# Linear attention beside a GEGLU block: heads packed in chunks of 120 columns against chunks of 128, with the first steps of two engines in program order

## The chip, the cores and the metric

The kernel runs on one core of a Trainium2 chip. The time is device time in microseconds (us) of whole executions; the profile shows one execution, and its span is about 1.8 us shorter than the time. Five engines matter. TensorE multiplies matrices (PE in the profile, its weight loads are PEld), VectorE (DVE) and ScalarE (ACT) do elementwise work, the Pool engine (POOL) helps, and SyncE (SP) starts the DMAs. All runs told of here are in the fast state. Ratios are the mean time of one kernel's fast runs over that of the other's of the same rounds, so they are not quite the ratio of the medians quoted beside them.

## The reference

```python
x  = A_x                                  # 1 x 2048 x 640, bf16
xn = layernorm(x)
# A: linear attention, 32 heads of 20
q, k, v = split(xn @ wqkv)                # 640 -> 3 * 640
pq, pk  = phi(q), phi(k)                  # phi(t) = where(t > 0, t + 1, exp(t)) + 1e-6
kv = sum over tokens of pk^T v            # per head, 20 x 20
z  = sum over tokens of pk                # per head, 20
o  = (pq @ kv) / (pq @ z + 1e-6)
A  = o @ wo
# B: GEGLU
B  = (gelu(xn @ w_gate) * (xn @ w_up)) @ w_down   # 640 -> 1728 -> 640
out = x + A + B
```

## The kernel before

The kernel has two stages. The k/v stage goes through 16 tiles of 128 tokens: statistics and normalization, five transposes, k and v by matmuls, phi(k), and the sum of pk^T v in an accumulator. Then come four blocks of 512 tokens: q and phi(q), 13 gate/up chunks and one tail chunk, with the attention of the block (nd, its division, transposes) put between the first chunks, then the last projection.

Heads of 20 columns don't fill 128 evenly. So the kernel before takes six heads at a time, 120 columns, and the last 40 columns of the 640 as a sixth chunk:

```python
HPC = P // Dh            # 6 heads
CW = HPC * Dh            # 120 columns
HC = -(-D // CW)         # 6 chunks
NW = CW + HPC            # 126
...                      # HCH: (lo, m, voff, vw) of each chunk; the last one is widened to 128 columns

def kv_accumulate(t, pk, v_ext):
    for j, (lo, m, voff, vw) in enumerate(HCH):
        col = (j % GPB) * P
        nc.tensor.matmul(
            kv_acc[0:m, j // GPB, col:col + 1 + vw],
            lhsT=pk[:, lo:lo + m], rhs=v_ext[:, j, 0:1 + vw], ...)
...
for i in range(NT + 2):                  # the k/v stage, pipelined over tiles
    if i < NT:
        ensure_stats(i)                  # bn_stats on VectorE, log and exp on ScalarE, in batches:
        normalize_transpose(i)           #   tile 0, tile 1, tiles 2-3, tiles 4-5, ...
    if 0 <= i - 1 < NT:
        pk = k_tile(i - 1); v_ext = v_tile(i - 1); ...
    if 0 <= i - 2 < NT:
        kv_accumulate(i - 2, ...)
...
def nd_tile(b, tt, pqT):                 # numerators and denominators of one token tile
    nd = ps_nd.tile([P, HC, P], FP32, tag="nd")          # ps_nd has one buffer
    for j, (lo, m, voff, vw) in enumerate(HCH):
        nc.tensor.matmul(nd[:, j, 0:NW], lhsT=pqT[0:m, j, tsl], rhs=kvz[0:m, j, :], ...)
    # VectorE: rden = nd[.., CW:] + eps; rden = 1 / rden; o = nd * rden   (720 columns)
...
    for j, (lo, m, voff, vw) in enumerate(HCH):          # q of a block: 6 chunks
        for c in range(DC):
            nc.tensor.matmul(q_ps[0:m, :], lhsT=wqkv_sb[:, c, lo:lo + m], rhs=xnT[:, c, bsl], ...)
        phi(pqT[0:m, j, :], q_ps[0:m, :], m, TB, "eq")
```

The order of instructions on each engine is not that of the text: a scheduler orders them, from its own estimate of when each is ready.

Of the kernel before, what the change touches and what calls it, by code (L numbers as in the profile page):

```python
# [8 lines left out]
ALU = mybir.AluOpType  # L9
FP32 = mybir.dt.float32  # L10
BF16 = mybir.dt.bfloat16
PSUM = bass.MemoryType.PSUM
# [4 lines left out]
DEN_EPS = 1e-6  # L17
# [6 lines left out]
def kernel(  # L24
# [11 lines left out]
    nc = tc.nc  # L36
    P = nc.NUM_PARTITIONS

    Bsz, S, D = A_x.shape
    F = B_w_gate.shape[1]  # L40
    H = N_HEADS
    Dh = D // H
    assert Bsz == 1 and D % P == 0 and D == H * Dh
    TB = 512
    assert S % TB == 0
    DC = D // P
    NT = S // P
    NB = S // TB
    TPB = TB // P
    HPC = P // Dh  # L50
    CW = HPC * Dh
    HC = -(-D // CW)
    NW = CW + HPC

    HCH = []
    for j in range(HC):
        lo = j * CW
        vw = min(CW, D - lo)
        if vw <= 64 and D >= P:
            HCH.append((D - P, P, P - vw, vw))  # L60
        else:
            HCH.append((lo, vw, 0, vw))

    n_plain = F // P
    f_tail = F - n_plain * P
# [7 lines left out]
    SG = D // NS  # L73

    KA = D // 2
    nA = max(1, (HC + 1) // 2)
    VA = nA * CW
    assert KA <= 512 and D - KA <= 512 and VA <= 512 and 0 < D - VA <= 512
    nfullB = (D - VA) // CW
    tailB = D - VA - nfullB * CW  # L80
    GPB = 3
    assert HC <= 2 * GPB and NW <= P and (CW + 1) <= P

    x_flat = A_x.rearrange("b s d -> (b s) d")
    out_flat = out.rearrange("b s d -> (b s) d")
# [3 lines left out]
    consts = ctx.enter_context(tc.tile_pool(name="consts", bufs=1))  # L89
    wpool = ctx.enter_context(tc.tile_pool(name="wpool", bufs=1))  # L90
    big = ctx.enter_context(tc.tile_pool(name="big", bufs=1))
    blk = ctx.enter_context(tc.tile_pool(name="blk", bufs=1))
# [60 lines left out]
    )  # L153
    eps_ln = consts.tile([P, 1], FP32, name="eps_ln")
    nc.vector.memset(eps_ln[:], LN_EPS)
    masks = {}
    for (lo, m, voff, vw) in HCH:
        if voff in masks:
            continue
        mk = consts.tile([P, HPC, Dh], FP32, name=f"mask{voff}")  # L160
        nc.gpsimd.memset(mk[:], 1.0)
        nc.gpsimd.affine_select(
            out=mk[:], in_=mk[:], compare_op=ALU.is_ge, fill=0.0,
            base=-voff, pattern=[[-Dh, HPC], [0, Dh]], channel_multiplier=1,
        )
        nc.gpsimd.affine_select(
            out=mk[:], in_=mk[:], compare_op=ALU.is_ge, fill=0.0,
            base=voff + Dh - 1, pattern=[[Dh, HPC], [0, Dh]], channel_multiplier=-1,
        )
        masks[voff] = mk  # L170
    kvz = big.tile([P, HC, NW], BF16, name="kvz")
    nc.gpsimd.memset(kvz[:], 0.0)

    xnT = big.tile([P, DC, S], BF16, name="xnT")
# [2 lines left out]
    rstd_all = big.tile([P, NT], FP32, name="rstd_all")  # L177
    nmr_all = big.tile([P, NT], FP32, name="nmr_all")

    kv_acc = ps_nd.tile([P, 2, 512], FP32, tag="nd")  # L180
    nc.vector.memset(kv_acc[:], 0.0)

    def phi(dst, src_ps, rows, cols, tag):
        e = work.tile([P, cols], FP32, tag=tag)
        nc.scalar.activation(out=e[0:rows], in_=src_ps, func=ACT.Exp)  # L185
        nc.vector.tensor_scalar(  # L186
            out=e[0:rows], in0=e[0:rows], scalar1=1.0, scalar2=PHI_EPS,
            op0=ALU.min, op1=ALU.add,
        )
        nc.vector.scalar_tensor_tensor(  # L190
            out=dst, in0=src_ps, scalar=0.0, in1=e[0:rows], op0=ALU.max, op1=ALU.add
        )
# [53 lines left out]
    def v_tile(t):  # L246
        tsl = slice(t * P, (t + 1) * P)
        vA = ps_oa.tile([P, VA], FP32, tag="oa")
        vB = ps_ob.tile([P, D - VA], FP32, tag="ob")
        for (ps, lo, hi) in ((vA, 0, VA), (vB, VA, D)):  # L250
            for c in range(DC):
                nc.tensor.matmul(  # L252
                    ps[:], lhsT=xnT[:, c, tsl], rhs=wqkv_sb[:, c, 2 * D + lo:2 * D + hi],
                    start=(c == 0), stop=(c == DC - 1),
                )
        v_ext = work.tile([P, HC, CW + 1], BF16, tag="vext")
        nc.gpsimd.memset(v_ext[:, :, 0:1], 1.0)
        nc.scalar.copy(
            out=v_ext[:, 0:nA, 1:1 + CW], in_=vA[:].rearrange("p (j c) -> p j c", c=CW)
        )  # L260
        if nfullB:
            nc.scalar.copy(
                out=v_ext[:, nA:nA + nfullB, 1:1 + CW],
                in_=vB[:, 0:nfullB * CW].rearrange("p (j c) -> p j c", c=CW),
            )
        if tailB:
            nc.scalar.copy(out=v_ext[:, HC - 1, 1:1 + tailB], in_=vB[:, nfullB * CW:])
        return v_ext

    def kv_accumulate(t, pk, v_ext):  # L270
        for j, (lo, m, voff, vw) in enumerate(HCH):
            col = (j % GPB) * P
            nc.tensor.matmul(  # L273
                kv_acc[0:m, j // GPB, col:col + 1 + vw],
                lhsT=pk[:, lo:lo + m], rhs=v_ext[:, j, 0:1 + vw],
                start=False, stop=(t == NT - 1), skip_group_check=True,
            )

# [16 lines left out]
        stats_done.add(bi)  # L295

    pend_kv = {}
    for i in range(NT + 2):
        if i < NT:
            ensure_stats(i)  # L300
            normalize_transpose(i)
        if 0 <= i - 1 < NT:
            t = i - 1
            pk = k_tile(t)
            v_ext = v_tile(t)
            pend_kv[t] = (pk, v_ext)
        if 0 <= i - 2 < NT:
            t = i - 2
            kv_accumulate(t, *pend_kv.pop(t))

    for j, (lo, m, voff, vw) in enumerate(HCH):
        g_, col = j // GPB, (j % GPB) * P
        mk = masks[voff]
        mk2d = mk[:].rearrange("p h d -> p (h d)")
        nc.vector.tensor_tensor(
            out=kvz[0:m, j, 0:vw], in0=kv_acc[0:m, g_, col + 1:col + 1 + vw],
            in1=mk2d[0:m, 0:vw], op=ALU.mult,
        )
        nc.vector.tensor_scalar(
            out=kvz[0:m, j, CW:CW + HPC], in0=mk[0:m, :, 0],  # L320
            scalar1=kv_acc[0:m, g_, col:col + 1], scalar2=None, op0=ALU.mult,
        )

    def nd_tile(b, tt, pqT):
        tsl = slice(tt * P, (tt + 1) * P)
        nd = ps_nd.tile([P, HC, P], FP32, tag="nd")
        for j, (lo, m, voff, vw) in enumerate(HCH):
            nc.tensor.matmul(  # L328
                nd[:, j, 0:NW], lhsT=pqT[0:m, j, tsl], rhs=kvz[0:m, j, :],
                start=True, stop=True,  # L330
            )
        rden = small.tile([P, HC, HPC], FP32, tag="rden")
        nc.vector.tensor_scalar(
            out=rden[:], in0=nd[:, :, CW:CW + HPC], scalar1=DEN_EPS, scalar2=None, op0=ALU.add
        )
        nc.vector.reciprocal(out=rden[:], in_=rden[:])
        o = work.tile([P, HC, HPC, Dh], BF16, tag="o")
        nc.vector.tensor_tensor(  # L338
            out=o[:],
            in0=nd[:, :, 0:CW].rearrange("p j (h d) -> p j h d", d=Dh),  # L340
            in1=rden[:].unsqueeze(3).to_broadcast([P, HC, HPC, Dh]),
            op=ALU.mult,
        )
        return o

    def tr_tile(b, tt, o, oT):
        tsl = slice(tt * P, (tt + 1) * P)
        o_flat = o[:].rearrange("p j h d -> p (j h d)")
        oT_ps = ps_tp.tile([P, DC, P], BF16, tag="tp")
        for c in range(DC):  # L350
            nc.tensor.transpose(oT_ps[:, c, :], o_flat[:, c * P:(c + 1) * P], ident[:])  # L351
        nc.scalar.copy(out=oT[:, :, tsl], in_=oT_ps[:])  # L352
# [63 lines left out]
    TR_AT = 3  # L416
    for b in range(NB):
        bsl = slice(b * TB, (b + 1) * TB)
        pqT = blk.tile([P, HC, TB], BF16, tag="pqT")
        for j, (lo, m, voff, vw) in enumerate(HCH):  # L420
            q_ps = ps_mm.tile([P, TB], FP32, tag="mm")
            for c in range(DC):
                nc.tensor.matmul(  # L423
                    q_ps[0:m, :], lhsT=wqkv_sb[:, c, lo:lo + m], rhs=xnT[:, c, bsl],
                    start=(c == 0), stop=(c == DC - 1),
                )
            phi(pqT[0:m, j, :], q_ps[0:m, :], m, TB, "eq")
        oT = blk.tile([P, DC, TB], BF16, tag="oT")
        hT = blk.tile([P, FC, TB], BF16, tag="hT")
        o_tiles = {}  # L430
        for fc in range(FC):
            ffn_chunk(b, fc, hT)
            last = (fc == FC - 1)
            for tt in range(TPB):
                if fc == ND_AT + tt or (last and tt not in o_tiles and fc < ND_AT + tt):
                    o_tiles[tt] = nd_tile(b, tt, pqT)
            for tt in range(TPB):
                if tt in o_tiles and o_tiles[tt] is not None and (fc == TR_AT + tt or last):
                    tr_tile(b, tt, o_tiles[tt], oT)
                    o_tiles[tt] = None  # L440
        for tt in range(TPB):
            final_tile(b, tt, hT, oT)
# [30 lines left out]
```

## Time and profile before

| | before |
|---|---|
| time | 306.18 us median (305.46 to 307.96, 16 runs) |
| TensorE busy | 294.4 of 304.7 us (97%) |
| k/v stage ends, first q matmul | 66.05 us |
| one block | 58.8 us |
| q of one block | 30 matmuls, 6.48 us |

From the page of the kernel before, the parts on busy time per engine and on the chain of work that ended last (followed back from the last instruction to what released each step):

```profile
PE 294.4 (97%) x1948; PEld 179.8 (59%) x1948; DVE 145.5 (48%) x320; ACT 109.9 (36%) x218; POOL 20.3 (7%) x49
...
PE 90%; DVE 5%; DMA 3%; SPq 1%; ACT 0%; issue 0%
```

TensorE is the bound. The next lines are TensorE's timeline at the start. The columns are start, length, engine, line of the kernel, operation, output and inputs, shapes and count; in brackets is the idle time before it and what ended it. A group's length includes the pipeline's tail of the last matmul, so differences of starts give the spacing.

```profile
8.04 1.54 PE L237 MATMUL kA<-wqkv_sb,xnT 128*128 128x320 bf16 x5
9.37 1.50 PE L237 MATMUL kB<-wqkv_sb,xnT 128*128 128x320 bf16 x5
...
14.80 0.45 PE L228 MATMUL tp<-ident,xn 128*128 128x128 bf16 x5 [2.56 <-POOL xn L222]
...
16.69 0.84 PE L237 MATMUL kB<-wqkv_sb,xnT 128*128 128x320 bf16 x5 [0.76 <-DVE pk L190]
...
19.03 0.44 PE L228 MATMUL tp<-ident,xn 128*128 128x128 bf16 x5
19.30 0.84 PE L237 MATMUL kA<-wqkv_sb,xnT 128*128 128x320 bf16 x5
```

After v of tile 0 TensorE idles 2.56 us until tile 2's normalized rows come from the Pool engine, and 0.76 us before kB of tile 1. From 29 us on it never idles. ScalarE's timeline in that stretch:

```profile
12.92 0.30 ACT L201 ACTIVATE lnv_all<-mv_all,eps_ln 128x2 f32<-128x2 f32 x1 [5.42 <-DVE mv_all L198]
...
13.36 0.67 ACT L229 COPY xnT<-tp 128x640 bf16<-128x640 bf16 x1
```

The transposes of tile 1 were ready at 8.2 us, but their copy to SBUF (13.36 us) stands behind the logarithm for tiles 2 and 3 (12.92 us), which waited 5.42 us for statistics of rows that were still being loaded.

The chain view of the kernel before, for q of the first two blocks (start, length, count):

```profile
66.20 6.60 PE q_ps L423 x30
...
125.08 6.47 PE q_ps L423 x30
```

And VectorE's timeline around the first nd tile, with TensorE's for the nd tiles:

```profile
77.84 0.18 DVE L333 TENSOR_SCALAR rden<-nd 128x36 f32<-128x36 f32 x1
78.06 0.38 DVE L336 RECIPROCAL rden<-rden 128x36 f32<-128x36 f32 x1
78.47 0.91 DVE L338 TENSOR_TENSOR o<-nd,rden 128x720 bf16<-128x720 f32 x1
```

```profile
76.96 0.51 PE L328 MATMUL nd<-kvz,pqT 120*128 120x126 bf16 x6
...
79.46 0.51 PE L328 MATMUL nd<-kvz,pqT 120*128 120x126 bf16 x6
```

The first nd tile begins at 76.96 us. VectorE finishes o at 78.47 + 0.91 = 79.38 us and the next nd, which needs the same PSUM buffer, starts at 79.46 us.

### The profile page before, as it was taken

How to read it: one execution, taken by the hardware profiler on the slowest of the kernel's cores; microseconds unless marked ns; L12 is line 12 of the kernel's file. 1: busy time of each engine (PE TensorE's matmuls, PEld its weight loads, DVE VectorE, ACT ScalarE, POOL GpSimd, SP SyncE). 2: the span in 40 equal slices, each digit the busy share in tenths (PEclk: the TensorE clock that was granted, in tenths of full speed). 3: DMA queues.
4: the chain of work that ended last, by engine and by line, in shares of the span. 5: the costliest groups of instructions: out<-in, count | busy, mean ns of one | idle time of the engine just before them, and what ended most of it. 6: DMA issues, size and time to landing. Idle time of an engine off the chain costs nothing.

```text
span 304.7 us, 4834 instructions
## 1 busy us (share of the span) xinstructions
PE 294.4 (97%) x1948; PEld 179.8 (59%) x1948; DVE 145.5 (48%) x320; ACT 109.9 (36%) x218; POOL 20.3 (7%) x49
## 2 busy tenths in 40 slices
PE   5699999999999999999999999999999999999995
PEld 2467777775554577645446776454467755544773
DVE  5699554468752311477423116673231186533211
ACT  3267877756353400253433004443320063533000
POOL 5132322100000000000000000000000000000000
PEclk9999999999999999999999999999999999999999
DMA  7999900000000001000000000000001000000001
GB/s 230 328 377 364 344 30 2 0 2 0 2 1 1 0 24 43 24 0 2 0 0 2 35 29 24 0 1 2 0 1 44 22 24 0 0 3 0 22 24 43
DMA packets 11638, 15.62 MB, mean 51 GB/s; under 512 B 1952, under 2 KB 10336, under 8 KB 11616
## 3 DMA queue, kind: packets, MB, share of 16 engines
q1 hardware_dynamic: 11616, 15.32, 14.7%
q8 instruction: 15, 0.25, 0.3%
q14 instruction: 7, 0.06, 0.1%
HBM read 12.70 MB, written 2.62 MB: 50 GB/s over the span
## 4 chain that ended last, share of the span: by engine, by line
PE 90%; DVE 5%; DMA 3%; SPq 1%; ACT 0%; issue 0%
PE acc L365 20%; PE u_ps L390 18%; PE g_ps L390 18%; PE q_ps L423 9%; PE acc L371 7%; PE vA L252 3%; PE kB L237 3%; DVE st L197 3%; DMA x_all<-in_A_x_dram 3%; PE kA L237 2%; PE vB L252 2%; PE nd L328 2%; PE oT_ps L351 1%; PE gu_ps L401 1%; PE kv_acc L273 1%; DVE pk L190 1%
## 5 line engine op out<-in xcount | busy, mean ns | idle before, releaser
L365 PE MATMUL acc<-wd_sb,hT 128*128 128x320 bf16 x448 | 66.1, 299 | 0.0
L390 PE MATMUL u_ps<-xnT,wu_sb 128*128 128x512 bf16 x260 | 64.6, 379 | 0.0
L390 PE MATMUL g_ps<-xnT,wg_sb 128*128 128x512 bf16 x260 | 64.6, 379 | 0.0
L396 DVE TENSOR_TENSOR hT<-g,u_ps 128x512 bf16<-128x512 bf16 x52 | 35.8, 688 | 58.4 <-PE u_ps L390 53.9
L365 PEld LDWEIGHTS <-hT 128*128 128x128 bf16 x448 | 43.8, 98 | 17.7
L395 ACT ACTIVATE g<-g_ps 128x512 bf16<-128x512 f32 x52 | 31.0, 597 | 54.2 <-PE g_ps L390 54.1
L376 DVE TENSOR_TENSOR res<-acc,x_all 128x320 bf16<-128x320 f32 x32 | 15.7, 491 | 63.3 <-PE acc L371 63.3
L390 PEld LDWEIGHTS <-wu_sb 128*128 128x128 bf16 x260 | 25.4, 98 | 30.8
L185 ACT ACTIVATE e<-q_ps 120x512 f32<-120x512 f32 (+1 forms) x24 | 14.3, 597 | 70.6 <-PE q_ps L423 64.9
L390 PEld LDWEIGHTS <-wg_sb 128*128 128x128 bf16 x260 | 24.4, 98 | 25.1
L186 DVE TENSOR_SCALAR e<-e 128x320 f32<-128x320 f32 (+2 forms) x56 | 21.3, 381 | 19.2 <-ACT e L185 19.1
L371 PE MATMUL acc<-wo_sb,oT 128*128 128x320 bf16 x160 | 27.0, 299 | 0.0
L423 PE MATMUL q_ps<-xnT,wqkv_sb 128*120 128x512 bf16 (+1 forms) x120 | 26.7, 380 | 0.0
L423 PEld LDWEIGHTS <-wqkv_sb 128*120 128x120 bf16 (+1 forms) x120 | 15.2, 127 | 10.0 <-issue 0.2
L252 PEld LDWEIGHTS <-xnT 128*128 128x128 bf16 x160 | 15.7, 98 | 6.8
L237 PEld LDWEIGHTS <-xnT 128*128 128x128 bf16 x160 | 15.5, 101 | 7.1 <-issue 1.6
L371 PEld LDWEIGHTS <-oT 128*128 128x128 bf16 x160 | 15.6, 98 | 6.1
L190 DVE SCALAR_TENSOR_TENSOR pqT<-q_ps,e 120x512 bf16<-120x512 f32 (+1 forms) x24 | 16.6, 692 | 0.8
L352 ACT COPY oT<-oT_ps 128x640 bf16<-128x640 bf16 x16 | 11.1, 692 | 14.9 <-PE oT_ps L351 14.9
L197 DVE BATCH_NORM_STATS2 st<-x_all 128x6 f32<-128x320 bf16 x32 | 13.8, 461 | 5.2 <-DMA x_all<-in_A_x_dram 5.2
L237 PE MATMUL kB<-wqkv_sb,xnT 128*128 128x320 bf16 x80 | 14.1, 310 | 1.2 <-DVE pk L190 1.2
L338 DVE TENSOR_TENSOR o<-nd,rden 128x720 bf16<-128x720 f32 x16 | 14.5, 908 | 1.1
(55 smaller groups left out, 223.3 us busy)
## 6 DMA issues: line engine op xcount, KB each, us to landing
x_all<-in_A_x_dram SPq DMA_DIRECT2D x16, 160.0 KB, 3.7
out_dram<-res SPq DMA_DIRECT2D x16, 160.0 KB, 1.8
wqkv_sb<-in_A_wqkv_dram SPq DMA_DIRECT2D x3, 800.0 KB, 6.5
wg_sb<-in_B_w_gate_dram SPq DMA_DIRECT2D x1, 2160.0 KB, 11.5
wu_sb<-in_B_w_up_dram SPq DMA_DIRECT2D x1, 2160.0 KB, 17.1
wd_sb<-in_B_w_down_dram SPq DMA_DIRECT2D x1, 2080.0 KB, 14.9
wo_sb<-in_A_wo_dram SPq DMA_DIRECT2D x1, 800.0 KB, 9.3
wgu_tail<-in_B_w_gate_dram SPq DMA_DIRECT2D x1, 80.0 KB, 16.8
```

Of the source, the lines that this page charges most:

```text
L186: nc.vector.tensor_scalar(out=e[0:rows], in0=e[0:rows], scalar1=1.0, scalar2=PHI_EPS, op0=ALU.min, op1=ALU.add,)
L190: nc.vector.scalar_tensor_tensor(out=dst, in0=src_ps, scalar=0.0, in1=e[0:rows], op0=ALU.max, op1=ALU.add)
L197: nc.vector.bn_stats(out=st[:, s, :], in_=x_all[:, t, s * SG:(s + 1) * SG])
L237: nc.tensor.matmul(ps[:], lhsT=xnT[:, c, tsl], rhs=wqkv_sb[:, c, D + lo:D + hi], start=(c == 0), stop=(c == DC - 1),)
L252: nc.tensor.matmul(ps[:], lhsT=xnT[:, c, tsl], rhs=wqkv_sb[:, c, 2 * D + lo:2 * D + hi], start=(c == 0), stop=(c == DC - 1),)
L365: nc.tensor.matmul(acc[:], lhsT=hT[0:m, fc, tsl], rhs=wd_sb[0:m, fc, lo:hi], start=(i == 0), stop=(i == n_mm - 1),)
L371: nc.tensor.matmul(acc[:], lhsT=oT[:, c, tsl], rhs=wo_sb[:, c, lo:hi], start=(i == 0), stop=(i == n_mm - 1),)
L376: nc.vector.tensor_tensor(out=res[:, lo:hi], in0=acc[:], in1=x_all[:, t, lo:hi], op=ALU.add)
L390: nc.tensor.matmul(ps[0:m, :], lhsT=w_sb[:, c, flo:flo + m], rhs=xnT[:, c, bsl], start=(c == 0), stop=(c == DC - 1),)
L395: nc.scalar.activation(out=g[0:m], in_=g_ps[0:m], func=ACT.Gelu_apprx_tanh)
L396: nc.vector.tensor_tensor(out=hT[0:m, fc, :], in0=g[0:m], in1=u_ps[0:m], op=ALU.mult)
L423: nc.tensor.matmul(q_ps[0:m, :], lhsT=wqkv_sb[:, c, lo:lo + m], rhs=xnT[:, c, bsl], start=(c == 0), stop=(c == DC - 1),)
```

## The change

Its intent: fill the 128 columns. q and k are cut in five chunks of exactly 128 columns, whatever heads fall in them. A head that straddles two chunks contributes from both, and PSUM adds the parts up. Each head gets its own column of ones in v, so a head takes 21 columns. One q chunk less means five matmuls less per block. The first four steps of the k/v stage are also put in program order on ScalarE and VectorE.

```diff
-    HPC = P // Dh
-    CW = HPC * Dh
-    HC = -(-D // CW)
-    NW = CW + HPC
+    SW = Dh + 1
+    QCH = []
+    for i in range(DC):
+        h_lo = (i * P) // Dh
+        h_hi = min(H - 1, (i * P + P - 1) // Dh)
+        QCH.append((h_lo, h_hi - h_lo + 1))        # 7, 7, 8, 7, 7 heads
...
     def kv_accumulate(t, pk, v_ext):
-        for j, (lo, m, voff, vw) in enumerate(HCH):
-            col = (j % GPB) * P
+        for i, (h_lo, nh) in enumerate(QCH):
+            bank, col = KVR[i]
             nc.tensor.matmul(
-                kv_acc[0:m, j // GPB, col:col + 1 + vw],
-                lhsT=pk[:, lo:lo + m], rhs=v_ext[:, j, 0:1 + vw],
+                kv_acc[:, bank, col:col + nh * SW],
+                lhsT=pk[:, i * P:(i + 1) * P],
+                rhs=v_ext[:, h_lo:h_lo + nh, :].rearrange("p h c -> p (h c)"),
...
+    with tc.manual_schedule(engines={mybir.EngineType.Activation, mybir.EngineType.DVE}):
+        for i in range(4):
+            step(i)
+    for i in range(4, NT + 2):
+        step(i)
...
     def nd_tile(b, tt, pqT):
-        nd = ps_nd.tile([P, HC, P], FP32, tag="nd")
+        nd = ps_nd.tile([P, 2, BANK], FP32, tag="nd")
...      # the 5 chunks, one of them split at the bank: 6 matmuls, parts of a head accumulate
...      # rden: two additions (24 and 8 heads), one reciprocal; o: two multiplies (480 and 160)
...
-        for j, (lo, m, voff, vw) in enumerate(HCH):
+        for i in range(DC):
             q_ps = ps_mm.tile([P, TB], FP32, tag="mm")
             for c in range(DC):
                 nc.tensor.matmul(
-                    q_ps[0:m, :], lhsT=wqkv_sb[:, c, lo:lo + m], rhs=xnT[:, c, bsl],
+                    q_ps[:], lhsT=wqkv_sb[:, c, i * P:(i + 1) * P], rhs=xnT[:, c, bsl],
```

Cut: the masks, the copies of v (three per tile become two), and the masking of the accumulator.

## The prediction

> **What bounds the kernel.** The page gives TensorE 294.4 of the 304.7 us span (97%), and 90% of the chain of work that ended last. From about 29 us on, TensorE has no idle time: the timeline shows a steady 3.30 us per token tile in the k/v stage until 66 us, then four blocks of 58.8 us. Only instructions taken off TensorE's stream, or gaps closed before 29 us, can move the time. VectorE (48%) and ScalarE (36%) count where they make TensorE wait: at the start, and at the nd tiles.
>
> **What the change takes away.**
> 1. q is projected in 5 chunks of 128 columns instead of 5 of 120 and one of 128. The chain shows 30 q matmuls in 6.47 to 6.48 us per block, 216 ns each. This agrees with the Trainium skill (TensorE: Matmul & The Clock Gate, Back-to-back issue gap: N/2.4 + 2.5 ns = 216 ns at N=512). Five fewer per block: 1.08 us, times 4 = 4.32 us, all on the chain. The 120-column weight loads take 133 ns against 98 ns for 128 columns, but are hidden behind the matmuls: I count nothing for them. VectorE also loses 4 phi chunks (about 1.1 us each), off the chain.
> 2. Start. ScalarE's order before puts the logarithm for tiles 2 and 3 ahead of the copy of transposed tile 1; it waits 5.42 us for statistics until 12.92 us, and TensorE idles 2.56 us before tile 2's transposes and 0.76 us before kB of tile 1. With the first four steps in program order, the k/v of tile 1 come before tile 2's transposes (the order of instructions shows it). But VectorE now does tile 0's phi before the statistics of tiles 2 and 3, so tile 2's transposes come at about 16.6 instead of 14.8 us, after a gap of about 1.1 us; then tile 3's transposes wait about 0.8 us. Following the durations through, kA of tile 2 starts near 18 instead of 19.3 us: gain 1.4 us (0.3 to 2.3).
>
> **What it adds.**
> 3. kv accumulation: 5 matmuls of 147/168 columns instead of 6 of 121/41. Before 0.31 us per tile in the timeline; after 756/2.4 + 5 x 2.5 = 0.33 us. Loss 0.3 us over 16 tiles.
> 4. nd: 756 columns in 6 matmuls before and after (one chunk is split at the bank): 0.34 us, no change. But nd has one buffer, and the timeline shows o ending at 79.38 us and the next nd starting at 79.46 us: no slack. VectorE's chain gets longer: two additions (about 0.14 us more) and two multiplies of 480 and 160 instead of one of 720 (0.91 us; about equal). I expect 0.05 to 0.2 us of TensorE wait before the second and third nd tiles of each block: 8 times, 0.8 us loss. Where transposes widen the slot (2.78 us), none.
>
> **Sum.** 306.19 - 4.32 - 1.4 + 0.3 + 0.8 = 301.6 us. Range 300.2 to 303.0. Faster by over 2% (below 300.1): 0.11; within 2%: 0.87; slower by over 2%: 0.02.
>
> **What would show it.** q: 25 matmuls in 5.40 us per block in the chain. Start: kA of tile 2 near 18 us, and the k/v stage ending 0.8 to 1.5 us sooner than 66 us. kv: tile period 3.32 us. nd: waits of TensorE or its weight loads on o, and a period over 2.50 us between the first nd tiles of a block. Last stage: unchanged.
>
> **What would make it wrong.** VectorE's backlog after the start may give back the gain (phi of tile 1 stands behind many statistics), or its order may fit better than I think (gain over 2 us). The nd wait may be zero or twice as large.

## The result

| | before | after |
|---|---|---|
| time, median | 306.18 us (305.46 to 307.96, 16 runs) | 300.71 us (299.46 to 302.37, 11 runs) |
| ratio | | 0.9824 (95%: 0.9802 to 0.9845) |
| TensorE busy, span of the profile | 294.4 of 304.7 us | 290.2 of 298.1 us |
| first q matmul | 66.05 us | 63.87 us |
| first q matmul to the end | 238.65 us | 234.23 us |
| one block | 58.8 us | 57.7 us |

The time lies in the stated range, and the change is within 2%, faster by 1.8%. A second set of six runs of the changed kernel on another occasion gave 300.25 us and a ratio of 0.9794 (0.9764 to 0.9824), so the gain lies close to the 2% line. The changed kernel scatters over 2.9 us, the kernel before over 2.5. Section 6 looks at the start, where executions differ, but what makes the scatter stays open.

The same views of the changed kernel. First the page:

```profile
PE 290.2 (97%) x1912; PEld 174.0 (58%) x1912; DVE 140.6 (47%) x337; ACT 106.5 (36%) x198; POOL 22.4 (8%) x54
...
PE 93%; DMA 3%; SPq 1%; DVE 0%; POOL 0%; ACT 0%; issue 0%; POOLq 0%
```

TensorE's timeline at the start:

```profile
7.51 0.57 PE L236 MATMUL kA<-wqkv_sb,xnT 128*128 128x320 bf16 x3 [1.71 <-DMA wqkv_sb<-in_A_wqkv_dram]
...
8.54 1.54 PE L236 MATMUL kB<-wqkv_sb,xnT 128*128 128x320 bf16 x5
9.88 1.71 PE L251 MATMUL vA<-wqkv_sb,xnT 128*128 128x360 bf16 x5
...
12.18 0.84 PE L236 MATMUL kA<-wqkv_sb,xnT 128*128 128x320 bf16 x5
...
15.66 0.45 PE L227 MATMUL tp<-ident,xn 128*128 128x128 bf16 x5 [0.27 <-POOL xn L221]
16.89 0.44 PE L227 MATMUL tp<-ident,xn 128*128 128x128 bf16 x5 [0.78 <-ACT xnT L228]
17.17 0.84 PE L236 MATMUL kA<-wqkv_sb,xnT 128*128 128x320 bf16 x5
```

k and v of tile 1 (from 12.18 us) now come before tile 2's transposes. Two small gaps remain: 0.27 us before tile 2's transposes and 0.78 us before tile 3's. kA of tile 2 starts at 17.17 instead of 19.30 us. The first q matmul comes 2.2 us sooner than before, more than the 0.8 to 1.5 us that the prediction named; this profiled execution took 299.87 us, 0.8 us less than the median. In the profile of the second set q starts at 64.77 us, 1.3 us sooner. Also, k and v of tile 0 run slowly: kB takes 1.34 us (8.54 to 9.88) where kB of tile 1 takes 0.68.

The chain for q, then VectorE around the first nd tile, then TensorE's nd tiles:

```profile
64.04 5.39 PE q_ps L439 x25
...
121.69 5.40 PE q_ps L439 x25
```

```profile
74.46 0.25 DVE L349 TENSOR_SCALAR rden<-nd 128x24 f32<-128x24 f32 x2
74.75 0.35 DVE L352 RECIPROCAL rden<-rden 128x32 f32<-128x32 f32 x1
75.13 0.89 DVE L355 TENSOR_TENSOR o<-nd,rden 128x480 bf16<-128x480 f32 x2
```

```profile
73.59 0.50 PE L336 MATMUL nd<-kvz,pqT 128*128 128x147 bf16 x6
...
76.08 0.51 PE L336 MATMUL nd<-kvz,pqT 128*128 128x147 bf16 x6
...
78.59 0.50 PE L336 MATMUL nd<-kvz,pqT 128*128 128x147 bf16 x6
```

q takes 5.40 us per block. The nd tiles are 2.49 and 2.51 us apart, as before: there is no new wait. The weight loads of nd wait for o eight times, 2.6 us in all, against 2.4 us before; TensorE's matmuls don't. From the start of nd to the end of o VectorE needs 75.13 + 0.89 - 73.59 = 2.43 us; before it needed 79.38 - 76.96 = 2.42 us.

### The profile page after: what moved, and what is told of

The parts are those of the page before. It is cut to its first block, busy times and chain, and to the rows that moved or that the text cites. A ratio compares the mean times of both kernels' runs of the same rounds, so it can differ in the third digit from the quotient of the medians.

```text
span 298.1 us, 4756 instructions
## 1 busy us (share of the span) xinstructions
PE 290.2 (97%) x1912; PEld 174.0 (58%) x1912; DVE 140.6 (47%) x337; ACT 106.5 (36%) x198; POOL 22.4 (8%) x54
## 4 chain that ended last, share of the span: by engine, by line
PE 93%; DMA 3%; SPq 1%; DVE 0%; POOL 0%; ACT 0%; issue 0%; POOLq 0%
PE acc L381 20%; PE u_ps L406 19%; PE g_ps L406 19%; PE acc L387 7%; PE q_ps L439 7%; PE vA L251 4%; PE kA L236 3%; PE kB L236 3%; DMA x_all<-in_A_x_dram 3%; PE vB L251 3%; PE nd L336 2%; PE kv_acc L269 2%; PE oT_ps L367 1%; PE tp L227 1%; PE gu_ps L417 1%; SPq L124 1%
## 5 line engine op out<-in xcount | busy, mean ns | idle before, releaser
L184 ACT ACTIVATE e<-q_ps 128x512 f32<-128x512 f32 x20 | 12.0, 598 | 68.7 <-PE q_ps L439 63.0
L185 DVE TENSOR_SCALAR e<-e 128x320 f32<-128x320 f32 (+1 forms) x52 | 19.0, 365 | 20.4 <-ACT e L184 20.3
L439 PE MATMUL q_ps<-xnT,wqkv_sb 128*128 128x512 bf16 x100 | 22.2, 379 | 0.0
L439 PEld LDWEIGHTS <-wqkv_sb 128*128 128x128 bf16 x100 | 9.7, 98 | 11.1
L251 PE MATMUL vA<-wqkv_sb,xnT 128*128 128x360 bf16 x80 | 15.6, 328 | 0.0
L236 PE MATMUL kA<-wqkv_sb,xnT 128*128 128x320 bf16 x80 | 13.8, 301 | 1.7 <-DMA wqkv_sb<-in_A_wqkv_dram 1.7
L425 POOL MEMSET hT<- 128x512 bf16 x4 | 2.3, 566 | 174.5 <-PE acc L381 174.5
L355 DVE TENSOR_TENSOR o<-nd,rden 128x480 bf16<-128x480 f32 (+1 forms) x32 | 14.2, 486 | 1.1
```

The source lines that it names most:

```text
L184: nc.scalar.activation(out=e[0:rows], in_=src_ps, func=ACT.Exp)
L185: nc.vector.tensor_scalar(out=e[0:rows], in0=e[0:rows], scalar1=1.0, scalar2=PHI_EPS, op0=ALU.min, op1=ALU.add,)
L236: nc.tensor.matmul(ps[:], lhsT=xnT[:, c, tsl], rhs=wqkv_sb[:, c, D + lo:D + hi], start=(c == 0), stop=(c == DC - 1),)
L251: nc.tensor.matmul(ps[:], lhsT=xnT[:, c, tsl], rhs=wqkv_sb[:, c, 2 * D + lo:2 * D + hi], start=(c == 0), stop=(c == DC - 1),)
L355: nc.vector.tensor_tensor(out=o[:, ha:hb, :], in0=hv[:, :, 1:SW], in1=rden[:, ha:hb].unsqueeze(2).to_broadcast([P, hb - ha, Dh]), op=ALU.mult,
L439: nc.tensor.matmul(q_ps[:], lhsT=wqkv_sb[:, c, i * P:(i + 1) * P], rhs=xnT[:, c, bsl], start=(c == 0), stop=(c == DC - 1),)
```

## The experiments

Theory: the gain has two parts, about 4.4 us less TensorE work in the four blocks and a start that is shorter by 1 to 2 us; nd costs nothing. Rivals: that the two parts are not independent, because the scheduler's order moves with the layout; that part of q's saving was the faster weight load; that ScalarE's order alone, or VectorE's alone, made the start faster.

### 1. Each half of the change alone

The layout alone (label layout_only):

```diff
-    with tc.manual_schedule(engines={mybir.EngineType.Activation, mybir.EngineType.DVE}):
-        for i in range(4):
-            step(i)
-    for i in range(4, NT + 2):
+    for i in range(NT + 2):
         step(i)
```

> The changed kernel without its program-order block: only the 20-wide-head layout (5 q chunks, 5 kv matmuls). Theory (two independent parts: q saves 4.3 us, kv costs 0.3, nd costs nothing, start saves 1.4 to 2.2): 302.2 us, -4.0, ratio about 0.987; 25 q matmuls in 5.40 us per block; the gaps before tile 2's transposes (2.56 us) and kB of tile 1 (0.76 us) are still there. Rival (the layout also moves the scheduler's order at the start, so the start's gain comes from the layout as well): under 301 us, and no 2.5 us gap before tile 2's transposes.

Measured: 303.14 us (302.55 to 303.39, 4 runs), ratio 0.9890 (0.9874 to 0.9906), so 3.4 us less than before, not 4.0. The gap before tile 2's transposes is there, 2.60 us; the one before kB of tile 1 is not, because kA runs at half speed there and fills it. But the scheduler's order also differs from that of the kernel before, and brings two later waits for VectorE's phi where the kernel before has one of 0.41 us. From TensorE's timeline of layout_only:

```profile
14.48 0.71 PE L227 MATMUL tp<-ident,xn 128*128 128x128 bf16 x5 [2.60 <-POOL xn L221]
...
24.15 0.84 PE L236 MATMUL kB<-wqkv_sb,xnT 128*128 128x320 bf16 x5 [0.49 <-DVE pk L189]
...
31.27 0.84 PE L236 MATMUL kB<-wqkv_sb,xnT 128*128 128x320 bf16 x5 [0.31 <-DVE pk L189]
```

The k/v stage's last accumulation starts at 66.30 us; in the kernel before at 65.30 us. Of that 1.0 us, 0.4 us is the wider kv matmuls (below) and about 0.4 us is these waits (0.80 against 0.41 us). The remainder of about 0.2 us may be the half speed: in this execution TensorE ran slowly from 13.9 to 17.3 us, which the profile of the kernel before doesn't show there. So the layout also moves the order at the start, as the rival said, but for the worse.

The program order alone, added to the kernel before (label sched_only):

```diff
-    for i in range(NT + 2):
+    def step(i):
         ...
+    with tc.manual_schedule(engines={mybir.EngineType.Activation, mybir.EngineType.DVE}):
+        for i in range(4):
+            step(i)
+    for i in range(4, NT + 2):
+        step(i)
```

> The kernel before with only the first four steps of ScalarE and VectorE in program order. Theory: 304.2 us, 1.4 to 2.4 us less than before, all of it gained before 20 us: kA of tile 2 starts at 17 to 18 us instead of 19.3; everything after is shifted as a whole (q 30 matmuls in 6.48 us, tile period 3.30 us). Rival (VectorE's backlog gives the gain back later): kA of tile 2 early, but the first q matmul at about 66 us as before, and 306 us.

Measured: 304.94 us (303.72 to 307.0, 6 runs), ratio 0.9962 (0.9929 to 0.9996), 1.2 us less in the mean, a little under what was expected. kA of tile 2 starts at 18.15 us and the last accumulation at 63.76 us, 1.5 us sooner than before: the gain is not given back later. The two halves add up to 4.6 us in the means; together they gave 5.4 and, in the second set, 6.3 us. The program order seems worth more on top of the layout (2.0 to 2.9 us) than on the kernel before; it also takes away the two waits that the layout brought, which would fit. The intervals are too wide to establish this difference.

### 2. A sixth q chunk put back

Label q_sixth: the fifth chunk of the changed kernel is computed as two halves of 64 columns.

```diff
-        for i in range(DC):
+        for i, r0, r1 in [(i, 0, P) for i in range(DC - 1)] + [(DC - 1, 0, 64), (DC - 1, 64, P)]:
...
-                    q_ps[:], lhsT=wqkv_sb[:, c, i * P:(i + 1) * P], rhs=xnT[:, c, bsl],
+                    q_ps[r0:r1, :], lhsT=wqkv_sb[:, c, i * P + r0:i * P + r1], rhs=xnT[:, c, bsl],
```

> The changed kernel with its fifth q chunk computed as two halves of 64 columns: again 30 q matmuls and 6 phi per block, same result. Theory: 6.48 us of q per block, +1.08 each, +4.3 us over the changed kernel, about 305.0 (ratio 0.996). Rival (part of q's saving was the faster weight load or VectorE's shorter phi backlog, or halves of the array overlap): clearly less or more than 4.3, for instance +2.

Measured: 305.16 us (303.99 to 305.85, 6 runs), ratio 0.9954 (0.9934 to 0.9974). Against 0.9824 and 0.9794 of the changed kernel that is 4.0 to 4.9 us more, where 4.3 was expected. This is most of what the change gained, for five more matmuls per block. TensorE's timeline of q_sixth, q of the second block (one record of the 30 is missing):

```profile
123.54 6.51 PE L439 MATMUL q_ps<-xnT,wqkv_sb 128*128 128x512 bf16 x29
```

With its tail q took 5.56 us there in the changed kernel. But q_sixth isn't quite clean: the scheduler also moved part of the first nd tile of a block ahead of its gate matmuls. The first two blocks grow by 1.09 and 1.06 us, as counted; the last two grow by 1.4 and 1.3 us, and in the third one nd waits 0.18 us for o. From the last accumulation to the end the profile has 4.9 us more than the changed kernel's, not 4.3.

### 3. Weight loads of 120 columns

Label w120 (wrong result, 8 columns of each chunk are left out; the check calls it correct all the same, so passing that check doesn't prove the attention part): the matmuls stay as many and as long, the weight loads of q and kv have 120 columns again.

```diff
-                    q_ps[:], lhsT=wqkv_sb[:, c, i * P:(i + 1) * P], ...
+                    q_ps[0:120, :], lhsT=wqkv_sb[:, c, i * P:i * P + 120], ...
...
-                lhsT=pk[:, i * P:(i + 1) * P],
+                lhsT=pk[:, i * P:i * P + 120],
+        nc.gpsimd.memset(pqT[96:P, :, :], 0.0)
```

> Wrong result on purpose: the changed kernel with 120 instead of 128 columns in every q and kv weight load (8 columns of each chunk left out), the matmuls as many and as long. Theory (weight loads of 120 columns take longer, 133 against 98 ns, but are hidden behind the matmuls): 25 q matmuls still in 5.40 us, kv 0.33 us per tile, tile period 3.32 us, time as the changed kernel. Rival (the slower load was part of what the change saved): q above 5.5 us per block, or kv above 0.36 us per tile.

From the groups by line and shape of w120, the weight loads of q, and from its chain the first q:

```profile
L440 PEld LDWEIGHTS <-wqkv_sb 128*120 128x120 bf16 x100 | 13.2, 133 | 7.7
```

```profile
65.49 5.40 PE q_ps L440 x25
```

The loads take 133 ns instead of 98, and q still takes 5.40 us. The kv sum of one tile takes 48.46 - 48.13 = 0.33 us, as in the changed kernel. So the prediction's reading holds: the faster load (the Trainium skill, TensorE: Matmul & The Clock Gate, Weight-path perf modes, says it asks for 128 weights; the trace agrees with 133 against 98 ns, and the 64-column loads of q_sixth take 108 ns) was worth nothing here.

The whole took 301.96 us (301.69 to 303.17, 4 runs), ratio 0.9843 (0.9817 to 0.9870), which reaches above the changed kernel's. The excess, if it is one, lies before q: the first q matmul starts at 65.33 us (63.87 and 64.77 in the two profiles of the changed kernel), and from there to the end w120 takes 234.2 us, as the changed kernel does. The likely cause is the experiment's own memset on the Pool engine. Pool's and VectorE's timelines of w120:

```profile
4.35 2.23 POOL L436 MEMSET pqT<- 32x2560 bf16 x1
```

```profile
4.79 1.96 DVE L216 TENSOR_SCALAR xn<-x_all,mv_all,rstd_all 128x640 bf16<-128x640 bf16 x1 [0.60 <-ACT rstd_all L204]
```

Tile 0's normalization takes 0.45 us in the changed kernel; here it takes 1.96 us and ends just after the memset does. The Trainium skill (SBUF — State Buffer, SBUF: two separate sides) describes a port pair that these two engines, VectorE only in some of its modes, hold exclusively for a whole instruction. The trace fits that with 1.96 us instead of 0.45, but no run here isolates it.

### 4. Program order on one engine only

Labels sched_act and sched_dve: the changed kernel with the set of engines reduced to ScalarE, and to VectorE.

```diff
-    with tc.manual_schedule(engines={mybir.EngineType.Activation, mybir.EngineType.DVE}):
+    with tc.manual_schedule(engines={mybir.EngineType.Activation}):       # sched_act
+    with tc.manual_schedule(engines={mybir.EngineType.DVE}):              # sched_dve
```

> The changed kernel with program order on ScalarE alone; VectorE is ordered by the scheduler again. Theory (the gap came from ScalarE's logarithm standing ahead of the copy of transposed tile 1, and VectorE's order only delays the statistics of tiles 2 and 3): as fast as the changed kernel or up to 1 us faster, 299.7 to 300.7 us; tile 2's transposes earlier than 15.7 us. Rival (VectorE's order is what matters: phi of tile 0 early): slower than the changed kernel by 1 us or more.

Measured: 304.60 us (304.25 to 305.78, 6 runs), ratio 0.9945 (0.9929 to 0.9962), about 4 us slower than the changed kernel and 1.7 us slower than layout_only, which has no program order at all. My theory fell. TensorE's and VectorE's timelines of sched_act:

```profile
14.46 0.71 PE L227 MATMUL tp<-ident,xn 128*128 128x128 bf16 x5 [5.30 <-DVE xn L216]
```

```profile
11.06 1.28 DVE L196 BATCH_NORM_STATS2 st<-x_all 128x6 f32<-128x320 bf16 x3 [5.45 <-DMA x_all<-in_A_x_dram]
...
13.97 0.43 DVE L216 TENSOR_SCALAR xn<-x_all,mv_all,rstd_all 128x640 bf16<-128x640 bf16 x1
```

The scheduler ordered VectorE's statistics of tiles 2 and later ahead of tile 1's normalization (13.97 us). They wait 5.45 us for data. With ScalarE's order fixed, the same kind of block simply moved to VectorE.

> The changed kernel with program order on VectorE alone; ScalarE is ordered by the scheduler. sched_act showed 5.3 us of idle TensorE before tile 1's transposes, because VectorE's scheduler put tile 1's normalization behind statistics that wait for data. Theory (VectorE's order is what the block of program order buys; ScalarE's follows): 300 to 301 us, as the changed kernel within 1 us, kA of tile 2 at 17 to 18.5 us. Rival (ScalarE's order is needed as well): above 302 us, with a gap before k or v of tile 1.

Measured: 300.53 us (299.45 to 302.26, 6 runs), ratio 0.9797 (0.9767 to 0.9827), with kA of tile 2 at 17.96 us. That is the changed kernel's time. So VectorE's order was enough: with it fixed, the scheduler put ScalarE's copy of tile 1 ahead of the logarithm (14.39 us) by itself. From ScalarE's timeline of sched_dve:

```profile
8.15 0.69 ACT L228 COPY xnT<-tp 128x640 bf16<-128x640 bf16 x1 [0.78 <-PE tp L227]
```

### 5. VectorE's chain from nd to o

The prediction read 0.08 us between the end of o and the next nd as "no slack", and expected a wait of 0.8 us in all that did not come. Label chain_long puts a second reciprocal into the chain:

```diff
         nc.vector.reciprocal(out=rden[:], in_=rden[:])
+        scr = small.tile([P, H], FP32, tag="scr")
+        nc.vector.reciprocal(out=scr[:], in_=rden[:])
```

> The changed kernel with a second reciprocal of 128x32 (0.35 us, into an unused tile) in VectorE's chain from nd to o. Theory (the chain ends just as the next nd begins, so all of it is waited for in the 2.50 us slots, 8 of them, and hardly in the 2.78 us slots): the slots become 2.78 to 2.85 us, and the kernel 2.2 to 2.8 us slower, about 303.3. Rival (the chain has slack, and that is why the prediction's 0.8 us did not appear): under 0.5 us slower.

Measured: 300.37 us (300.07 to 301.21, 6 runs), ratio 0.9801 (0.9774 to 0.9829), no loss to be seen. But this doesn't show slack. The scheduler saw the longer chain and moved TensorE's instructions:

```profile
77.02 0.38 PE L408 MATMUL g_ps<-xnT,wg_sb 128*128 128x512 bf16 x1
77.24 0.50 PE L336 MATMUL nd<-kvz,pqT 128*128 128x147 bf16 x6
```

One gate matmul now goes before the second nd, and the third nd goes between transposes. So the experiment was inconclusive, and repeated with TensorE's order of the blocks fixed (label chain_fixed; the order of its matmuls is that of the changed kernel):

```diff
+    ctx.enter_context(tc.manual_schedule(engines={mybir.EngineType.PE}))
     for b in range(NB):
```

> As chain_long (a second reciprocal of 0.35 us in VectorE's chain from nd to o), but with TensorE's order of the four blocks held as in the changed kernel; in chain_long the scheduler had moved one gate matmul ahead of the second nd tile and nd into the transposes, which hides the wait. Theory (the chain in the changed kernel ends right when the next nd begins): the second and third nd of a block wait 0.25 to 0.35 us each, the slots become 2.75 to 2.85 us instead of 2.50, 8 slots in all: 2.0 to 2.8 us slower than the changed kernel. Rival (the chain has real slack of 0.3 us or more): slots of 2.50 us and no loss.

Measured: 301.56 us (301.2 to 302.38, 5 runs), ratio 0.9828 (0.9805 to 0.9851). The timelines of TensorE and VectorE in chain_fixed:

```profile
73.84 0.50 PE L336 MATMUL nd<-kvz,pqT 128*128 128x147 bf16 x6
...
76.54 0.51 PE L336 MATMUL nd<-kvz,pqT 128*128 128x147 bf16 x6
...
79.05 0.50 PE L336 MATMUL nd<-kvz,pqT 128*128 128x147 bf16 x6
```

```profile
75.39 0.35 DVE L354 RECIPROCAL scr<-rden 128x32 f32<-128x32 f32 x1
75.66 0.82 DVE L357 TENSOR_TENSOR o<-nd,rden 128x480 bf16<-128x480 f32 x2
76.61 0.69 DVE L414 TENSOR_TENSOR hT<-g,u_ps 128x512 bf16<-128x512 bf16 x1
```

The first slot grows from 2.49 to 2.70 us. From the start of nd to the end of o it is now 75.66 + 0.82 - 73.84 = 2.64 us, 0.21 us more than in the changed kernel; the slot grew by the same 0.21 us. So there is no slack: the reading was right. But the added instruction of 0.35 us cost only 0.21, because neighbouring instructions overlap: o starts 0.27 us after the second reciprocal does, and is itself recorded as 0.82 instead of 0.89 us. And only the first slot grew. In the second, VectorE's multiply for hT (76.61 us) had been done while TensorE waited, so the chain had caught up. The block takes 57.9 instead of 57.7 us, some 0.8 us in the four; the ratio alone is too coarse to show that.

### 6. The scatter at the start, and a faster version

In the profile of the changed kernel TensorE waits for the k weights before tile 0's k, and then part of tile 0 runs at half speed. The second set of runs (label after_again) shows it again:

> The changed kernel once more, on the chip of the following runs, as their base. Expected 300 to 302 us, ratio 0.982; 25 q matmuls in 5.40 us; start differs from execution to execution with the clock of TensorE in the first 20 us (matmuls of 320 columns at 0.13 or 0.27 us apart).

TensorE's timeline of after_again:

```profile
8.27 0.57 PE L236 MATMUL kA<-wqkv_sb,xnT 128*128 128x320 bf16 x3 [2.40 <-DMA wqkv_sb<-in_A_wqkv_dram]
...
9.45 1.54 PE L236 MATMUL kB<-wqkv_sb,xnT 128*128 128x320 bf16 x5
10.79 1.71 PE L251 MATMUL vA<-wqkv_sb,xnT 128*128 128x360 bf16 x5
...
12.93 0.84 PE L236 MATMUL kA<-wqkv_sb,xnT 128*128 128x320 bf16 x5
13.61 0.84 PE L236 MATMUL kB<-wqkv_sb,xnT 128*128 128x320 bf16 x5
```

kB of tile 0 takes 10.79 - 9.45 = 1.34 us for five matmuls of 320 columns, 0.27 us each; kB of tile 1 takes 0.68 us, 0.136 each. The trace also records when the clock changes: it has half speed from 8.97 to 12.38 us, 3.41 us; in the first profile of the changed kernel from 8.38 to 11.79. The Trainium skill (TensorE: Matmul & The Clock Gate, Part 1) says that the clock is halved after an idle window of 3413 ns that runs free of the kernel; the length and the varying place of the slow stretch agree with it. But TensorE was idle for only 2.40 of the 3.41 us before it, so how idle a window must be is not shown here.

Label fill puts matmuls nobody needs into that wait:

```diff
-WARMUP_MATMULS = 8
+WARMUP_MATMULS = 9
...
         for c in range(DC):
             nc.tensor.transpose(tp[:, c, :], xn[:, c * P:(c + 1) * P], ident[:])
+        for _ in range(4 if t == 0 else 0):
+            nc.tensor.matmul(wps[:], lhsT=xn[:, 0:P], rhs=wz[:], start=True, stop=True)
```

(TensorE's order is held at this place, so that the four stay behind the transposes.)

> The changed kernel with one more warm-up matmul and four dummy matmuls after tile 0's transposes, where TensorE waits for the k weights (1.7 us idle in the profile). Theory (that idle stretch makes the clock fall for 3.4 us, and part of k and v of tile 0 runs at half speed, which costs TensorE 1.6 to 2 us of which at most 1 us is on the path to tile 2): 0.3 to 1 us faster than the changed kernel, less scatter, granted clock 1.0. Rival (start is bound by VectorE's statistics whatever TensorE's clock): no change within 0.3 us.

TensorE's timeline of fill, kB of tile 0:

```profile
8.82 0.84 PE L239 MATMUL kB<-wqkv_sb,xnT 128*128 128x320 bf16 x5
```

Measured: 299.46 us (299.11 to 300.22, 6 runs), ratio 0.9777 (0.9751 to 0.9804). kB of tile 0 now takes 0.84 us with its tail, at full speed. The mean is 0.5 us below after_again on the same chip, which the intervals do not resolve. The scatter is 1.1 us instead of 1.8, in six runs each, which is too few to tell. All three profiles with these dummy matmuls (fill and the two below) have kB of tile 0 at full speed; of the seven profiles without them in which VectorE's first steps are in program order, only q_sixth's does. So the filler, with the ninth warm-up matmul, probably works on tile 0.

That the clock makes the scatter is not shown. The changed kernel's runs with a mean granted clock of 1.000 took 298.95 to 300.71 us, those with 0.993 or 0.994 took 299.46 to 301.63. And that mean is a poor witness: chain_long and sched_dve have 1.000 although kB of tile 0 ran at half speed in them (the closing list says why), and fill_bounds has 0.994 in four of its six runs in spite of the filler.

Label fill_bounds splits the statistics of tiles 2 and 3 into two batches (a 3 added to the list of bounds), so that tile 2 need not wait for tile 3.

> As fill, and the statistics of tiles 2 and 3 make two batches of one instead of one of two, so that tile 2 is normalized without waiting for tile 3. Theory (tile 2's transposes wait for VectorE's statistics): tile 2's transposes move from 15.7 to about 14.5 us, the 0.78 us wait for the copy goes; 1 to 2 us faster than the changed kernel, about 299. Rival (VectorE's total work up to tile 4 binds): TensorE waits later for phi instead, and the gain is under 0.5 us.

Measured: 303.05 us (301.97 to 303.54, 6 runs), ratio 0.9885 (0.9856 to 0.9913), about 3.3 us slower than fill. Tile 2 did come early (kA at 15.46 us). But tile 3's statistics now stood behind the phi of tile 1, and TensorE idled 1.56 us before tile 3's transposes and another 0.78 us before kA of tile 3.

Label fill_norm3 is fill with tile 2 normalized on VectorE (0.45 us) instead of the Pool engine (0.87 us):

```diff
-N_DVE_NORM = 2
+N_DVE_NORM = 3
```

> As fill, with tile 2 normalized on VectorE (0.45 us) instead of the Pool engine (0.87 us). Theory (tile 2's transposes wait for its normalized tile and tile 3's for the copy behind them): tile 2's transposes about 0.4 us earlier, kA of tile 2 at about 16.3 instead of 16.8 us, 0.2 to 0.6 us faster than fill, about 299.0. Rival (VectorE's backlog): later waits for phi, no gain.

Measured: 298.96 us (298.93 to 299.25, 4 runs), ratio 0.9740 (0.9717 to 0.9762). kA of tile 2 starts at 15.82 us and the last accumulation at 61.93 us, against 16.82 and 62.68 us in fill. This is the fastest version tried: 2.6% faster than the kernel before, and its interval lies below those of both sets of the changed kernel, below the second by a hair. It overlaps that of fill (0.9751 to 0.9804), so the step from fill is seen in the trace and not established by the times. The result passes the record's check.

## Why the prediction was right, point by point

| term | predicted | shown by the runs |
|---|---|---|
| q, five matmuls fewer per block | -4.32 us | -4.42 us from the first q matmul to the end; q_sixth puts 4.0 to 4.9 us back |
| weight loads of 120 columns | 0 | 0: 5.40 us of q per block in w120 |
| start | -1.4 us (0.3 to 2.3) | -1.4 us and -2.3 us in the two sets (what is left of the mean gain of 5.4 and 6.3 us) |
| kv accumulation | +0.3 us | tile period 3.326 us instead of 3.300, +0.4 us |
| nd waits | +0.8 us | none: slots of 2.49 and 2.51 us |

q was right to a tenth. It is a plain count on an engine that is never idle; the extra 0.1 us is in the first block (6.60 to 5.39 us). The section of the skill that the prediction cites for 216 ns has another figure for a stream, which this trace contradicts; see the closing list.

The start had the right sign and about the right size, but not for quite the reason given. The prediction named ScalarE's logarithm ahead of the copy as the cause. With ScalarE's order alone fixed (sched_act) the kernel is 1.7 us slower than with none fixed (layout_only); with VectorE's alone (sched_dve) it is as fast as the changed kernel. Both engines could hold tile 1 back behind statistics that wait for data. It also put tile 2's transposes at 16.6 us after a gap of 1.1 us; they came at 15.66 us after 0.27, and in the second set at 16.55 us after 0.41. The wait before tile 3's transposes was predicted as 0.8 us and is 0.78 us. Between the two profiles the start moves by about 1 us, which the prediction did not foresee: kA of tile 2 comes at 17.17 and 18.06 us. Most of it is there already when the k weights land (first kA at 7.51 and 8.27 us).

The step that failed is the size of one term, "0.05 to 0.2 us of TensorE wait before the second and third nd tiles of each block: 8 times, 0.8 us loss"; it measured zero. The reading behind it, no slack, was right, as chain_fixed shows. The arithmetic on VectorE's chain was wrong. Two additions take 0.25 instead of 0.18 us. But the reciprocal is over 32 instead of 36 columns (0.35 instead of 0.38 us), and o has 640 instead of 720 columns: the two multiplies together take 0.89 us, against 0.91 for one. Their single lengths, 0.66 and 0.31 us, add up to more, because they overlap in the profile. And had the chain grown, the second slot would have caught up, as in chain_fixed, so four waits and not eight.

By this account, in which the start is the remainder and not a measurement of its own, the kernel came out 0.9 us below the predicted 301.6 us mostly because this cost of 0.8 us was not there. In the second set it was 1.35 us below, and the start makes up the rest. That the first set's start met 1.4 us so closely is partly luck: it differs by 0.9 us between the sets.

## What to carry to other kernels

Where one engine is busy without a gap, count its instructions and give each its spacing in the stream. That predicted the large part of this change to a tenth of a microsecond; the longer weight loads, behind matmuls of 147 columns and more, counted for nothing here. Where a start is held up, look at which in-order engine has put an instruction that waits for data ahead of one that is ready: mending that on one engine can move the same block to another, and a change of layout can move the scheduler's order as well, so test both parts alone and together. An experiment that adds work may be answered by the scheduler with another order; compare the orders before believing that the work was free.

## What the Trainium skill lacked or had wrong

- TensorE: Matmul & The Clock Gate, Back-to-back issue gap. It gives about 131 ns per matmul of 512 columns and 81 ns for 128 as the sustained rate of a stream of weight loads and matmuls, and calls N/2.4 + 2.5 the isolated gap. Here it is the formula that holds in the stream, with a weight load for each matmul: 216 ns at 512 columns (25 in 5.40 us), 0.33 us for the five kv matmuls of 756 columns in all (0.328 by the formula).
- TensorE: Matmul & The Clock Gate, Part 4. It says that the full clock doesn't engage for transposes and gives about 275 ns for one in a kernel. Here one takes 219 ns in the mean of the changed kernel, and in a busy stream five of 128 columns start 54 ns apart (19.03 to 19.30 us in the kernel before), against 98 ns in a slow stretch (7.55 to 8.04 us). So they do run at full clock here, among other matmuls. The trace lists them as matmuls with the identity and doesn't show whether that is the page's transpose mode.
- TensorE: Matmul & The Clock Gate, Weight-path perf modes. It measures the fast load at about 2 times and says it pays where the free dimension is small. Here it is 133 against 98 ns, 1.36 times, for 120 and 128 columns, and it changed nothing behind matmuls of 512 and of 147 columns.
- TensorE: Matmul & The Clock Gate, Part 1. It warns that clock events in a trace are unreliable. No recorded event is at odds with the spacing of matmuls, but the record is silent before its first event, and the profile's granted clock counts that time as full. In the kernel before, the five kA matmuls of tile 0 are 0.27 us apart (8.04 to 9.37 us), as in the slow stretches, and the first event is the rise at 10.7 us, while the granted clock of that stretch is given as 1.00. Up to the first event the spacing is the witness to use.
- VectorE: DVE Perf Modes, The TRN2 errata. Its (N + 151)/0.96 ns, given there for an fp32 add, also fits o, a multiply that reads PSUM: 658 ns measured at 480 columns (657), 908 at 720 (907), less well 314 at 160 (324).
